# Zero rows fill the MLP's remainder tile, so that all gate and up matmuls contract over 128 rows

## The chip, the core and the metric

The kernel runs on one core of one Trainium2 chip. The time is the device time of one launch in microseconds (us). Work is done by five engines with queues of their own: TensorE (PE, with its weight loads listed as PEld), VectorE (DVE), ScalarE (ACT), GpSimd (POOL) and SyncE (SP), which issues most transfers. ACT issues some transfers too.

## The reference

One transformer block with adaptive layer norm, one sequence of 2048 tokens, width D = 576, MLP width F = 4608, all in float32:

```python
mod = (silu(c) @ w_mod).reshape(1, 6, 1, 576)
sa, ca, ga, sb, cb, gb = (mod[:, i] for i in range(6))
h = layernorm(x) * (1 + ca) + sa
x = x + ga * attention(h)            # 32 heads, 16 key/value heads, last 512 cached positions
h = layernorm(x) * (1 + cb) + sb
gate, up = h @ W_gate, h @ W_up      # [2048, 576] @ [576, 4608]
return x + gb * ((max(gate, 0) * up) @ W_down)
```

## The kernel before

**Precision.** TensorE's inputs are of a rounded float32 type (`F32R`). An operand is kept as a high part (the rounded value) and a low part (what the rounding left), and a product is made of three: high x high, low x high, high x low.

**The MLP.** The contraction runs over the 576 channels. Gate and up are computed by a scheme of seven products in place of eight (Strassen's: `P1` to `P7`), so each of its halves has 288 channels: two tiles of 128 rows and a remainder of 32. There are 36 blocks (`m`), 18 over the first half of the tokens (the first pass) and 18 over the second, seven products in each, and for each product a matmul group for gate and one for up (`xx`). `prod` (line 943) issues a group: for each of the two tiles of 128 the three products of high and low parts, then one matmul for the remainder. That one holds all three in a single stack of rows: weights low, high, high against activations high, high, low, 32 rows each, which makes 96. The weights' tiles (`wop`, from `w_split` and `w_later`) have a fourth group of 32 rows with the high part once more; it is there, but not used.

**The activations.** The normed activations of the second layer norm are written to memory (`hb`, line 237), by `hb_store` (line 240). Its fifth part, the remainder, is stored three times over, 32 rows each, so that a load gives 96 rows. `hb_load` (line 250) loads a tile. From those loads the seven sums of the scheme (`B11`, `B21`, `B22`, `T1` to `T4`) are built for the first half of the tokens by `h0_load`, `h0_comb`, `h0_hi` and `h0_cut`, and for the second by `h_later`, which runs in the first pass beside the MLP; both split into high and low, and the rows 64 to 95 of a remainder become the low part. The results go to memory (`hkeep`) except three that stay on chip, and `h_back` reloads them as `hop` tiles, five transfers for each operand. Four operands are reloaded for the first pass, and seven for the second, all at the end of the first.

**Order.** PE, DVE, ACT and POOL execute in the order in which the program is written; attention's is written as steps with times (ten to a unit, 128 units), the MLP's as slots, seven to a block. In a slot stand one product of gate and up and one or two pieces of down projection (`md_piece`, line 599, 12 matmuls of 288 columns; `st_tile`, line 1045, 6 matmuls, in the second pass). SP's transfers follow the order of the program as well, and each waits in the queue for what it needs. Weights of the first pass are cut into high and low on the chip for each slot (`w_split`, lines 720 to 722) and kept; the second pass reloads them (`wop<-wk_P`, line 735). `w_sums` (line 750) makes sums of raw weights on DVE; line 610 adds a finished piece of down projection to the result.

Of the kernel before, what the change touches and what calls it, by code (L numbers as in the profile page):

```python
# [7 lines left out]
F32 = mybir.dt.float32  # L8
F32R = mybir.dt.float32r
# [5 lines left out]
P = 128  # L15
S = 2048
D = 576
# [5 lines left out]
NQB = S // 512  # L23
# [10 lines left out]
def kernel(  # L34
# [13 lines left out]
    nc = tc.nc  # L48
# [18 lines left out]
    dr = ctx.enter_context(tc.tile_pool(name="dr", bufs=1, space=bass.MemoryType.DRAM))  # L67
# [144 lines left out]
    def prep_out(d, k, src, key, slot=None, at=(None, "wC")):  # L212
# [11 lines left out]
        def cut():  # L224
# [9 lines left out]

    hT = [None] * NQB

    hb = {(qb, d): dr.tile([2, 3, 32, 512] if d == 4 else [P, 512], F32, name=f"hb{qb}_{d}")
          for qb in range(NQB) for d in range(5)}

    def hb_store(qb, d, cols, f, eng=None):  # L240
        eng = eng or nc.sync
        if d < 4:
            eng.dma_start(hb[qb, d][:, cols], f)
            return
        for j in range(2):
            s = f[32 * j:32 * j + 32]
            eng.dma_start(hb[qb, 4][j, :, :, cols].rearrange("r p n -> p r n"),
                              s[:, None, :].to_broadcast([32, 3, s.shape[1]]))

    def hb_load(dst, qb, j, t):  # L250
        if t < 2:
            nc.sync.dma_start(dst, hb[qb, 2 * j + t])
        else:
            nc.sync.dma_start(dst[:96], hb[qb, 4][j].rearrange("r p n -> (r p) n"))

    h0, late = {}, []
    pend, pend_act = [], []
# [483 lines left out]
    def w_sums(m, s):  # L741

        r = {ij: wraw.get((m, *ij)) for ij in RAW}
        if s == "S2":
# [8 lines left out]

    TERMS = {"B11": "+00", "B21": "+10", "T2": "+11-01+00", "T3": "+11-01", "T1": "+01-00",
             "T4": "+10-11+01-00", "B22": "+11"}
    hkeep = {(b, s, k): dr.tile([96 if k == 2 else P, 512], F32R, name=f"hk{b}_{s}_{k}")
             for b in range(2) for s in TERMS for k in range(5)}

    def terms_of(s, table):
        w = table[s]  # L760
        return [(w[i], int(w[i + 1]), int(w[i + 2])) for i in range(0, len(w), 3)]

    def h_later(b, s, t):

        st = {}
        n = 96 if t == 2 else P
        terms = terms_of(s, TERMS)

        def get(dst, j, k):
            hb_load(dst, 2 * b + k, j, t)  # L770

        def begin():
            if b:
                ab = wp.tile([P, 2, 512], F32, tag="wC", name=f"hx{b}_{s}_{t}")
                st["a"], st["b"] = ab[:, 0, :], ab[:, 1, :]
            else:
                for x in "ab":
                    st[x] = hp.tile([P, 512], F32, tag="hT", name=f"h{x}{b}_{s}_{t}")
            for x, term in zip("ab", terms):
                get(st[x], *term[1:])  # L780

        def comb(i):
            x, y = st["a"][:n], st["b"][:n]
            nc.gpsimd.tensor_tensor(x, x, y, op=ALU.add if terms[i][0] == "+" else ALU.subtract)  # L784
            if i + 1 < len(terms):
                get(st["b"], *terms[i + 1][1:])

        def cut():
            a = st["a"]
            hi = hp.tile([P, 512], F32R, tag="hT", name=f"hy{b}_{s}_{t}")  # L790
            nc.scalar.copy(hi[:n], a[:n])
            if t < 2:
                lo = st["b"].bitcast(F32R)
                nc.gpsimd.tensor_sub(lo, a, hi.bitcast(F32))
                stores.append((hkeep[b, s, 3 + t], lo))
            else:
                nc.gpsimd.tensor_sub(hi[64:96], a[64:96], hi[64:96].bitcast(F32))
            stores.append((hkeep[b, s, t], hi[:n]))

        return [begin] + [lambda i=i: comb(i) for i in range(1, len(terms))] + [cut]  # L800
# [6 lines left out]
    def h0_load(j, k, t):  # L807
        h0[j, k, t] = hp.tile([P, 512], F32, tag="hT", name=f"h0_{j}{k}{t}")
        hb_load(h0[j, k, t], k, j, t)

    def h0_comb(dst, a, b, op, t):
        n = 96 if t == 2 else P
        nc.vector.tensor_tensor(h0[(*dst, t)][:n], h0[(*a, t)][:n], h0[(*b, t)][:n], op=op)

    hy0 = {}

    def h0_hi(s, x, t):
        a, n = h0[(*x, t)], 96 if t == 2 else P
        hi = hy0[s, t] = hp.tile([P, 512], F32R, tag="hT", name=f"hy0_{s}_{t}")
        nc.scalar.copy(hi[:n], a[:n])  # L820

    def h0_here(s):
        for t in range(3):
            h0_hi(s, H0_CUT[s], t)
        for t in range(3):
            h0_cut(s, H0_CUT[s], t, True)

    def h0_cut(s, x, t, stay=False):
        a, n = h0[(*x, t)], 96 if t == 2 else P
        hi = hy0[s, t]  # L830
        if t < 2:
            lo = hy0[s, 3 + t] = hp.tile([P, 512], F32R, tag="hT", name=f"hz0_{s}_{t}")
            nc.gpsimd.tensor_sub(lo, a, hi.bitcast(F32))
        else:
            nc.vector.tensor_sub(hi[64:96], a[64:96], hi[64:96].bitcast(F32))
        if stay:
            if t == 2:
                hop[0, s] = [hy0[s, k] for k in range(5)]
            return
        if t < 2:  # L840
            stores.append((hkeep[0, s, 3 + t], lo))
        stores.append((hkeep[0, s, t], hi[:n]))

    def h_back(b, s):
        hs = hop[b, s] = [hp.tile([P, 512], F32R, tag="hT", name=f"hop{b}_{s}_{k}") for k in range(5)]
        for k in range(5):
            nc.sync.dma_start(hs[k][:96 if k == 2 else P].bitcast(F32), hkeep[b, s, k].bitcast(F32))


    WTERMS = {"P1": "+00", "P2": "+01", "P6": "+10+11-00", "P7": "+00-10", "P5": "+10+11", "P4": "+11",  # L850
# [83 lines left out]
    def prod(m, s, n, xx):  # L934

        hs, w = hop[m // NFP, OPS[s][1]], wop[n]
        ps = pair[m, s][:, xx, :]
        ops = []
        for t in range(2):
            ops += [(w[:, xx, t, :], hs[t]), (w[:, xx, 3 + t, :], hs[t]), (w[:, xx, t, :], hs[3 + t])]  # L940
        ops.append((w[0:96, xx, 2, :], hs[2][0:96]))
        for i, (a, c) in enumerate(ops):
            nc.tensor.matmul(ps, a, c, start=s not in heir(m) and i == 0 and s not in seeds_of(m), stop=i == len(ops) - 1,  # L943
                             skip_group_check=True)
# [164 lines left out]
    def heir(m):  # L1109
        return {"P2": "P1", "P3": "P5", **({"P4": "P7"} if 0 < m < NFP else {})}  # L1110

    def seeds_of(m):
        return ("P6", "P7") if 0 < m < NFP else ()
# [99 lines left out]
    def step(name, t, fn, *args):  # L1213
        sched.append((t + PLAN.get(name, 0), len(sched), fn, args))
# [14 lines left out]
    def setd(d, k, fn):  # L1229
        def go():  # L1230
            d[k] = fn()
        return go
# [119 lines left out]
    for i in range(1, first):  # L1352
        B = 80 * i
        for c, t, gap, a in (("q", 16, 5, 0), ("kv", 24, 5, 1), ("o", 44, 6, 2)):
            if parks[c] and i > a:
                key, d, pr = parks[c].pop(0)
# [7 lines left out]
    step("m3.col", 250, setd(mods, "b0", lambda: mod_col(3, 0.0)()))  # L1364
    step("m4.col", 400, setd(mods, "b", lambda: (mods["b0"], mod_col(4, 1.0)())))

    mkeep = dr.tile([P, D], F32, name="mkeep")

    def m5_back():
# [10 lines left out]
    for i, ab in enumerate(lay0 + lay):  # L1380
        n = i - len(lay0) - 2 * NFT + 4
# [125 lines left out]
    def after(t):  # L1507
        return next(x for x in calm if x >= t)

    t = 546  # L1510
    for s in ("P1", "P2", "P4", "P7", "P5", "P6", "P3"):
        for xx in range(2):
            for fn in w_later(s, xx, (xp, "xm", 640)):
                step("w.l", t, fn)
                t = after(t + 8)
# [18 lines left out]
    for t, s in ((1251, "B11"), (1257, "B21"), (1266, "T3")):  # L1534
        step("h.l", t, h_back, 0, s)
# [150 lines left out]
```

## Time and profile before

| | us |
|---|---|
| runs (3) | 2917.99 median, 2914.55 to 2919.14 |
| profiled execution, its own time | 2925.96 |
| its span, first to last instruction | 2923.5 |
| TensorE busy in it | 2858.1 |
| 0 to 1636 (mostly attention), TensorE busy | 1581.35 of 1636.00 |
| 1700 to 2290 (first pass of the MLP), TensorE busy | 584.10 of 590.00 |
| 2290 to 2840 (second pass), TensorE busy | 550.00 of 550.00 |

The mean granted clock of TensorE was 0.993 in that execution. In the profile, a row of grouped instructions gives line, engine, operation, output<-inputs by the program's names, shape, count, then busy time and mean nanoseconds of one, then the idle time of the engine before them with what ended it. A row of the timeline gives start, time taken, the same names, and how many alike in a row were merged. Matmuls overlap: one takes some 390 ns from start to its modelled end, and the next starts after some 227. The chain of waits is followed back from the last instruction, at each step to what released it.

### The profile page before, as it was taken

The numbers are of one execution on the slowest core, as the hardware profiler recorded it, in microseconds if no ns is written. First come the engines' busy times: TensorE is split into PE (matmuls) and PEld (weight loads), VectorE is DVE, ScalarE is ACT, GpSimd is POOL, SyncE is SP. The second block draws the span as 40 slices with busy tenths as digits, with TensorE's granted clock in tenths as the row PEclk, the third lists the DMA queues.
The fourth block names the chain that finished last, engine by engine and source line by source line (L and its number), as shares of the span: only waits on it lengthen the run. The fifth ranks groups of instructions, "written<-read, shape, count | busy, mean of one in ns | idle before, by whom it ended". The sixth has DMA issues, their size and how long they took to land. (4 is left out here: it accounts for less than half of the span.)

```text
span 2923.5 us, 41266 instructions
## 1 busy us (share of the span) xinstructions
PE 2858.1 (98%) x15214; PEld 2490.0 (85%) x15214; DVE 2161.4 (74%) x2981; ACT 1489.4 (51%) x2095; POOL 2117.4 (72%) x1564
## 2 busy tenths in 40 slices
PE   6799999999999999999999999999999999999999
PEld 4588888888888888888888888888888888888888
DVE  7888888888888888777889755666676466666666
ACT  4466666666676666666656444444444122222221
POOL 4588888888889889876778666777787356656553
PEclk9899999999999999999999999999999999999999
DMA  4011222222223223322144456666666944444443
GB/s 151 22 45 53 85 91 80 71 101 90 89 89 108 84 69 118 116 70 86 65 129 144 142 210 220 226 230 224 224 222 251 340 160 152 151 152 153 157 151 104
DMA packets 162697, 396.43 MB, mean 136 GB/s; under 512 B 14912, under 2 KB 61760, under 8 KB 162496
## 3 DMA queue, kind: packets, MB, share of 16 engines
q1 hardware_dynamic: 131472, 282.15, 30.2%
q10 hardware_dynamic: 31024, 111.65, 9.7%
q8 instruction: 120, 1.97, 0.3%
q14 instruction: 81, 0.66, 0.1%
HBM read 268.73 MB, written 153.32 MB: 144 GB/s over the span
## 5 line engine op out<-in xcount | busy, mean ns | idle before, releaser
L539 POOL TENSOR_TENSOR lo<-p,hi 128x1024 fp32r<-128x1024 f32 x256 | 610.0, 2405 | 1.1 <-ACT hi L519 1.1
L548 POOL TENSOR_TENSOR ks<-ks,p 128x512 f32<-128x512 f32 x256 | 344.0, 1344 | 271.8 <-ACT p L532 208.7
L460 DVE TRANSPOSE_TENSOR_REDUCE t<-s 128x32 f32<-128x1024 f32 x256 | 316.8, 1244 | 136.4 <-PE s L457 125.0
L943 PE MATMUL gu<-hop_B,wop 128*128 128x512 f32 (+1 forms) x1512 | 379.0, 394 | 0.9 <-DMA wop<-wk_P 0.9
L943 PEld LDWEIGHTS gu<-hop_B,wop 128*128 128x128 f32 (+1 forms) x1512 | 276.3, 188 | 53.6 <-issue 1.3
L383 PE MATMUL qps<-hTa,wA 128*128 128x512 f32 x1288 | 312.4, 394 | 9.7 <-ACT lfa L365 7.7
L943 PE MATMUL gu<-hop_T,wop 128*128 128x512 f32 (+1 forms) x1260 | 319.9, 393 | 0.0
L599 PE MATMUL wo<-woga,ohi 128*128 128x288 f32 x1472 | 305.9, 301 | 1.5 <-DVE lfa L363 1.5
L383 PEld LDWEIGHTS qps<-hTa,wA 128*128 128x128 f32 x1288 | 244.7, 190 | 62.1 <-ACT lfa L365 8.2
L530 DVE TENSOR_TENSOR p<-s,mb 128x1024 f32<-128x1024 f32 x246 | 290.3, 1219 | 4.1
L519 ACT CAST hi<-p 128x1024 fp32r<-128x1024 f32 x256 | 269.1, 1051 | 7.1
L599 PE MATMUL md<-wogb,hhi 128*128 128x288 f32 x1280 | 263.4, 298 | 5.8 <-DVE acc L610 4.9
L532 ACT ACTIVATE p<-p 128x1024 f32<-128x1024 f32 x246 | 259.9, 1056 | 8.0 <-DVE p L530 7.9
L943 PEld LDWEIGHTS gu<-hop_T,wop 128*128 128x128 f32 (+1 forms) x1260 | 228.4, 188 | 41.0
L610 DVE TENSOR_TENSOR acc<-md,acc 128x576 f32<-128x576 f32 x160 | 120.9, 756 | 177.5 <-PE md L599 177.1
L435 ACT ACTIVATE qhi<-qps 128x512 fp32r<-128x512 f32 x128 | 76.5, 598 | 341.1 <-PE qps L383 341.1
L599 PEld LDWEIGHTS wo<-woga,ohi 128*128 128x128 f32 x1472 | 238.7, 188 | 9.1 <-issue 1.9
L599 PEld LDWEIGHTS md<-wogb,hhi 128*128 128x128 f32 x1280 | 214.9, 190 | 19.1 <-DVE acc L610 6.3
L1054 DVE TENSOR_TENSOR acc<-st_P,acc 128x576 f32<-128x576 f32 x160 | 121.1, 757 | 133.7 <-PE st_P L1045 133.7
L599 PE MATMUL wo<-woga,olo 128*128 128x288 f32 x736 | 216.9, 295 | 0.3 <-POOL olo L588 0.2
L599 PE MATMUL md<-wogb,hlo 128*128 128x288 f32 x640 | 190.1, 297 | 0.0
L588 POOL TENSOR_TENSOR olo<-rb,ohi 128x512 fp32r<-128x512 f32 x128 | 167.3, 1307 | 23.6 <-ACT ohi L584 23.1
(269 smaller groups left out, 7106.6 us busy)
## 6 DMA issues: line engine op xcount, KB each, us to landing
wop<-wk_P SPq DMA_DIRECT2D x133, 640.0 KB
wk_P<-wop ACTq DMA_DIRECT2D x119, 640.0 KB
wr<-wlay SPq DMA_DIRECT2D x68, 384.0 KB
rogb<-wd SPq DMA_DIRECT2D x68, 288.0 KB
againq<-akq SPq DMA_DIRECT2D x18, 640.0 KB
rwA<-wq SPq DMA_DIRECT2D x32, 320.0 KB
wlay<-wg SPq DMA_DIRECT2D x36, 256.0 KB
roga<-wo SPq DMA_DIRECT2D x32, 288.0 KB
```

Of the source, the lines that this page charges most:

```text
L383: return [lambda i=i, a=a, b=b: nc.tensor.matmul(ps, a, b, start=(i == 0), stop=(i == n - 1)) for i, (a, b) in enumerate(ops)]
L460: nc.vector.tensor_reduce(t4[u][:, 2 * h:2 * h + 2, :].rearrange("p k b -> p (k b)"), t.rearrange("p k (b j) -> p (k b) j", j=32), axis=AX ...
L519: nc.scalar.copy(hi_[u, h], pt[u, h])
L530: nc.vector.tensor_tensor(p, t, bc[u][:, None, :].to_broadcast([P, 2, 512]), op=ALU.subtract)
L532: nc.scalar.activation(p, p, AF.Exp, bias=0.0, scale=1.0)
L539: nc.gpsimd.tensor_sub(lo_[u, h], pt[u, h], hi_[u, h].bitcast(F32))
L548: nc.gpsimd.tensor_tensor(ks_[u], ks_[u], p[:, j, :], op=ALU.add)
L588: nc.gpsimd.tensor_sub(olo[u], o.pop(u), ohi[u].bitcast(F32))
L599: nc.tensor.matmul(ps[:, half, :H2], a[:, sl], w[b][:, cs], start=(n == 0 and seed is None), stop=(n == 5), skip_group_check=seed is not None)
L610: nc.vector.tensor_tensor(av, ps[:, :, :H2], av, op=ALU.add)
L943: nc.tensor.matmul(ps, a, c, start=s not in heir(m) and i == 0 and s not in seeds_of(m), stop=i == len(ops) - 1, skip_group_check=True)
L1054: nc.vector.tensor_tensor(t, ps[:, :, :H2], t, op=ALU.add)
```

## The change

The stored remainder gets a fourth group of 32 rows. `hb_rest`, a new step at time 300 (unit 30 of attention), fills it with zeros, by eight transfers from a part of `wmod` that the launch code pads with zeros. `hb_load`, the sums and splits, `hkeep` and `h_back` handle 128 rows in place of 96, and the seventh matmul of every group contracts over 128 rows: the fourth group multiplies the repeated high part of the weights with zeros.

```diff
-    hb = {(qb, d): dr.tile([2, 3, 32, 512] if d == 4 else [P, 512], F32, name=f"hb{qb}_{d}")
+    hb = {(qb, d): dr.tile([2, 4, 32, 512] if d == 4 else [P, 512], F32, name=f"hb{qb}_{d}")
...
-            eng.dma_start(hb[qb, 4][j, :, :, cols].rearrange("r p n -> p r n"),
+            eng.dma_start(hb[qb, 4][j, 0:3, :, cols].rearrange("r p n -> p r n"),
...
+    def hb_rest():
+        for qb in range(NQB):
+            for j in range(2):
+                nc.sync.dma_start(hb[qb, 4][j, 3], wmod[0, 64:96, 4 * D:4 * D + 512])
...
-            nc.sync.dma_start(dst[:96], hb[qb, 4][j].rearrange("r p n -> (r p) n"))
+            nc.sync.dma_start(dst, hb[qb, 4][j].rearrange("r p n -> (r p) n"))
...
-    hkeep = {(b, s, k): dr.tile([96 if k == 2 else P, 512], F32R, name=f"hk{b}_{s}_{k}")
+    hkeep = {(b, s, k): dr.tile([P, 512], F32R, name=f"hk{b}_{s}_{k}")
...
-        n = 96 if t == 2 else P
+        n = P
...
-            nc.sync.dma_start(hs[k][:96 if k == 2 else P].bitcast(F32), hkeep[b, s, k].bitcast(F32))
+            nc.sync.dma_start(hs[k].bitcast(F32), hkeep[b, s, k].bitcast(F32))
...
-        ops.append((w[0:96, xx, 2, :], hs[2][0:96]))
+        ops.append((w[:, xx, 2, :], hs[2]))
...
+    step("hb.r", 300, hb_rest)
```

The line `n = 96 if t == 2 else P` changes in the same way in `h_later`, `h0_comb`, `h0_hi` and `h0_cut`. On PE, DVE, ACT and POOL every instruction stands where it stood. SP's queue is longer by eight rows. In unit 30 it reads, before (`wlay` is the relaid weights of the MLP, `wm` a part of the modulation weights, `rkv` and `roga` raw key/value and output weights; the brackets name what a row waits for):

```order
L189 DMA rwA_4441<-wq 128x640 [waits DMAHW4_49,DMAHW2_49,Pool_49]
L1383 DMA wlay<-wu 2x128x256 [waits DMAHW3_49]
L137 DMA wm_2_4566<-wmod 128x576 [waits DVE_49]
L1383 DMA wlay<-wg 2x128x256 [waits DMAHW5_49]
L203 DMA rkv_1_4597<-kv 128x512 [waits DMAHW6_49,DMAHW0_49,Pool_49]
```

and with the change (line numbers of the changed kernel):

```order
L189 DMA rwA_4441<-wq 128x640 [waits DMAHW4_49,DMAHW2_49,Pool_49]
L253 DMA hb_4_142<-wmod 32x512 [waits DMAHW3_49]
L253 DMA hb_4_142<-wmod 32x512
L253 DMA hb_4_147<-wmod 32x512 [waits DMAHW5_49]
L253 DMA hb_4_147<-wmod 32x512 [waits DMAHW6_49]
L253 DMA hb_4_152<-wmod 32x512 [waits DMAHW7_49]
L253 DMA hb_4_152<-wmod 32x512 [waits DMAHW0_49]
L253 DMA hb_4_157<-wmod 32x512 [waits DMAHW1_49]
L253 DMA hb_4_157<-wmod 32x512 [waits DMAHW2_49]
L1389 DMA wlay<-wu 2x128x256 [waits DMAHW3_49]
L137 DMA wm_2_4574<-wmod 128x576 [waits DMAHW4_49,DVE_49]
L1389 DMA wlay<-wg 2x128x256 [waits DMAHW5_49]
```

The eight transfers of zeros stand ahead of a `wlay` copy and of `wm`, each waiting for the earlier transfer that used its semaphore. The second place is the reload of an operand at the end of the first pass, on SP, before:

```order
L847 DMA hop_T_0_22755<-hk_T_0_372 128x512 [waits DMAHW6_49,Pool_49]
L847 DMA hop_T_1_22756<-hk_T_1_373 128x512 [waits DMAHW7_49,PE_49]
L847 DMA hop_T_2_22757<-hk_T_2_374 96x512 [waits DMAHW0_49,PE_49]
L847 DMA hop_T_3_22758<-hk_T_3_375 128x512 [waits DMAHW2_49,PE_49]
L847 DMA hop_T_4_22759<-hk_T_4_376 128x512 [waits DMAHW3_49,PE_49]
L735 DMA wop_22753<-wk_P_158 128x1280 [waits DMAHW4_49,PE_49]
```

and with the change:

```order
L852 DMA hop_T_0_22763<-hk_T_0_372 128x512 [waits DMAHW6_49,Pool_49]
L852 DMA hop_T_1_22764<-hk_T_1_373 128x512 [waits DMAHW7_49,PE_49]
L852 DMA hop_T_2_22765<-hk_T_2_374 128x512 [waits DMAHW0_49,PE_49]
L852 DMA hop_T_3_22766<-hk_T_3_375 128x512 [waits DMAHW2_49,PE_49]
L852 DMA hop_T_4_22767<-hk_T_4_376 128x512 [waits DMAHW3_49,PE_49]
L740 DMA wop_22761<-wk_P_158 128x1280 [waits DMAHW4_49,PE_49]
```

The rows and their waits are the same; the third transfer is of 128 rows in place of 96.

More of the change, by code (lines that the diff above doesn't have):

```diff
@@ L811, in h0_comb @@
     def h0_comb(dst, a, b, op, t):
-        n = 96 if t == 2 else P
+        n = P
         nc.vector.tensor_tensor(h0[(*dst, t)][:n], h0[(*a, t)][:n], h0[(*b, t)][:n], op=op)
@@ L817, in h0_hi @@
     def h0_hi(s, x, t):
-        a, n = h0[(*x, t)], 96 if t == 2 else P
+        a, n = h0[(*x, t)], P
         hi = hy0[s, t] = hp.tile([P, 512], F32R, tag="hT", name=f"hy0_{s}_{t}")
@@ L828, in h0_cut @@
     def h0_cut(s, x, t, stay=False):
-        a, n = h0[(*x, t)], 96 if t == 2 else P
+        a, n = h0[(*x, t)], P
         hi = hy0[s, t]
```

## The prediction

> **What bounds the kernel now.** First the page of the profile: the share of each engine, and the span in forty slices.
>
> ```profile
> PE 2858.1 (98%) x15214; PEld 2490.0 (85%) x15214; DVE 2161.4 (74%) x2981; ACT 1489.4 (51%) x2095; POOL 2117.4 (72%) x1564
> PE   6799999999999999999999999999999999999999
> PE 29%; POOL 2%; DMA 2%; DVE 1%; issue 1%; ACT 1%; ACTq 0%; SPq 0%; POOLq 0%; DVEq 0%
> ```
>
> TensorE is busy 98% of the span, and 9 tenths or more in every slice after the second. The change touches the MLP, which the matmuls of line 943 (1512 of them on `hop_B` alone) place from about 1636 us on. So the next view is the busy time by stage.
>
> ```profile
> core 0: us, PE busy (x) PEld busy (x) DVE busy (x) ACT busy (x) POOL busy (x), PEclk, DMA share, GB/s
> 1700.00:2290.00 590.00, 584.10 (x3197) 514.24 (x3196) 378.84 (x361) 253.28 (x353) 434.63 (x377) 0.99 0.64 231
> 2290.00:2840.00 550.00, 550.00 (x2952) 481.38 (x2953) 345.50 (x478) 129.46 (x243) 306.09 (x301) 1.00 0.51 170
> ```
>
> In the second pass of the MLP (2290 to 2840) TensorE has no idle time at all; in the first it has 590.00 - 584.10 = 5.9 us. What TensorE's own stream saves therefore comes off the end, except where something else holds it back. Where that is, the chain of waits tells, asked for 1876 to 2290 and then for 2290 to the end (it cannot be followed back past 1876).
>
> ```profile
> by line: PE gu L943 32.2%; PE md L599 20.4%; POOL wop L722 7.0%; issue 6.0%; POOL wop L721 3.8%; DVE ws L750 3.3%; DMA wk_P<-wop 3.0%; DVE wr L750 2.9%; DMA rogb<-wd 2.3%; DMA hx_T<-hb 2.3%; ACT wop L720 2.2%; DMA wop<-wk_P 2.0%; POOL hx_T
> by line: PE gu L943 64.5%; PE st_P L1045 28.5%; PE md L599 5.6%; DVE acc L610 0.2%; DVE su L1054 0.1%; DVE gu L1091 0.1%; DVE q L1092 0.1%; DVE acc L1066 0.1%; DVE q L1090 0.1%; issue 0.0%; DVEq L1091 0.0%; DVEq L610 0.0%
> ```
>
> In the second pass 98.6% of the chain is TensorE. In the first pass it is 52.6%; the other 47.4% of 414 us, about 196 us, runs through the cutting of weights on POOL, sums on DVE and transfers. TensorE is nearly always busy there too, but a faster TensorE would only wait a little longer at the next hand-over.
>
> **The matmul with fewer rows.** Each product of the MLP is seven matmuls into one bank, six with 128 rows and the last with 96. There are 36 blocks x 7 products x 2 (gate and up) = 504 of the last kind.
>
> ```profile
> L943 PE MATMUL gu<-hop_B,wop 128*128 128x512 f32 x1296 | 334.7, 393 | 0.9 <-DMA wop<-wk_P 0.9
> L943 PE MATMUL gu<-hop_B,wop 96*128 96x512 f32 x216 | 85.3, 395 | 0.0
> L383 PE MATMUL qps<-hTa,againq x504: 387/389/481, 1184.0 to 1617.4; 128*128 128x512 f32 x168
> ```
>
> Fewer rows buy nothing: 395 ns mean against 393 for its neighbours. And both stand above the 389 ns median of the same 128x512 form in the q projection, where no matmul has 96 rows. Ends of matmuls are modelled, so spacing of starts is the better measure. The timeline has a place where a 96-row matmul is followed by twelve of 128 rows and of the same width, with no wait between (second column: time taken, overlapping the next).
>
> ```profile
> 1648.48 0.39 PE L943 MATMUL gu<-hz_T,wop 128*128 128x512 f32 x1
> 1648.71 0.40 PE L943 MATMUL gu<-hy_T,wop 96*128 96x512 f32 x1
> 1648.94 0.40 PE L572 MATMUL pv<-hi,againv 128*128 128x512 f32 x1
> 1649.18 0.40 PE L573 MATMUL pv<-hi,againv 128*128 128x512 f32 x1
> 1649.41 0.39 PE L574 MATMUL pv<-lo,againv 128*128 128x512 f32 x1
> 1649.64 0.39 PE L572 MATMUL pv<-hi,againv 128*128 128x512 f32 x1
> ...
> 1651.45 0.39 PE L574 MATMUL pv<-lo,againv 128*128 128x512 f32 x1
> ```
>
> From 1649.64 to 1651.45 lie eight spacings: 1.81 / 8 = 0.2263 us each. From the 96-row matmul at 1648.71 to 1649.64 lie four: 0.93 us, that is 0.93 - 4 x 0.2263 = 0.025 us more. Getting into the 96 rows costs nothing (0.23); getting out disturbs that matmul and the next three. Is it the rows, or merely that one accumulation ends and the next begins with other operands? In attention the scores end and the q projection begins in another bank, all with 128 rows:
>
> ```profile
> 1002.05 0.39 PE L457 MATMUL s<-qlo,kv 128*128 128x512 f32 x1
> 1002.27 3.34 PE L383 MATMUL qps<-hTa,wA 128*128 128x512 f32 x14
> 1005.46 0.35 PE L483 MATMUL qm<-t,quad 128*128 128x80 f32 x2
> ```
>
> 0.22 us across the boundary, and fourteen in 3.19 us (0.228, the last being one before another change of form). So a boundary as such is free, and I put the 25 ns down to the change of rows. Two products in a row in the MLP, a piece of the chain, bear it out:
>
> ```profile
> 1980.56 3.22 PE gu L943 x14
> ```
>
> 3.22 us less 14 x 0.2263 = 3.17 leaves 0.05, twice 25 ns, and there are two 96-row matmuls in it. The page "TensorEngine Tiling (Array Packing)" of the Trainium skill says in its Key Properties that changing the tiling mode drains the engine; 96 rows is none of the modes that it lists, and it gives no time, so the sum does not use it, but the disturbance on leaving the 96 rows would be of that kind.
>
> **The price of one removal.** I take 26 ns: the 25 above, read to 10 ns, agrees with that within its rounding. The bounds come from the rest. Most of the 504 are followed not by matmuls of 512 columns but by a piece of down projection with 288, and whether the three disturbed spacings go away there is less sure:
>
> ```profile
> 2503.18 0.43 PE L1045 MATMUL st_P<-sw_B,sh_A 128*128 128x288 f32 x2
> ...
> 2503.99 1.79 PE L943 MATMUL gu<-hop_T,wop 128*128 128x512 f32 x7
> 2505.61 0.43 PE L1045 MATMUL st_P<-sw_B,sh_A 128*128 128x288 f32 x2
> 1007.29 0.39 PE L572 MATMUL pv<-hi,kv 128*128 128x512 f32 x1
> ...
> 1008.89 0.39 PE L573 MATMUL pv<-hi,kv 128*128 128x512 f32 x1
> ...
> 1010.03 0.42 PE L599 MATMUL wo<-woga,ohi 128*128 128x288 f32 x2
> ...
> 1010.82 0.29 PE L599 MATMUL wo<-woga,ohi 128*128 128x288 f32 x1
> ```
>
> In the MLP six of 288 columns and seven of 512 take 0.81 + 1.62 = 2.43 us; in attention, with 128 rows throughout, six take 0.79 and the first seven after such a piece take 1.60: 2.39. The difference, about 40 ns for each removal, is the upper bound; the lower is the 96-row matmul's own excess alone, 395 - 389 = 6 ns. So 504 removals save 504 x 0.026 = 13.1 us, at least 3.0 and at most 20.2. The seventh matmul itself goes on costing one spacing, as 128 rows do.
>
> **What is given back.** Three terms, all in the first pass.
> - Over the MLP (1636 to the end, 1287 us) 13.1 us is a rate of 1.0%. Where the chain is not TensorE's, 196 us, that gain becomes waiting: -2.0 us.
> - Before 1876 the chain is unknown for 240 us, worth 2.4 us; lost between nothing and all of it, I take half: -1.2 us.
> - Each of the eleven reloads of a cut operand from memory, and each load that builds one, carries 128 rows of 2 KB in place of 96, 64 KB more. It matters where transfers hold TensorE, which is at the end of the first pass, where seven reloads stand in one run of SP's queue:
>
> ```profile
> 2200.00:2290.00 90.00, 88.97 (x488) 78.11 (x487) 57.60 (x53) 36.15 (x50) 67.70 (x57) 1.00 0.78 280
> 2273.44 6.61 DMA hop_B<-hk_B
> 2281.46 8.29 DMA wop<-wk_P
> ```
>
> There the chain leaves TensorE for `hop_B` and then `wop`, and the 0.9 us wait quoted above on line 943 follows. Some four reloads lie ahead of that `wop`: 4 x 64 KB at the 280 GB/s of this stretch is 0.9 us; with what TensorE saves meanwhile, -1.0 us. Between 0 (the transfers have other slack) and 7 x 64 KB, 1.6 us.
>
> **What costs nothing, and its cover.** The eight new transfers of zeros (64 KB each) are put into SP's queue ahead of a `wlay` copy, in unit 30 of attention:
>
> ```profile
> 435.50 0.59 SPq L1383 DMA_DIRECT2D wlay<-wu  x1
> 443.12 0.34 SPq L137 DMA_DIRECT2D wm<-wmod  x1
> ```
>
> SP has nothing to issue from 436.1 to 443.1, 7.0 us, and eight issues of 0.34 to 0.59 take 2.7 to 4.7 us. Behind them stand that copy, `wm`, and the next key/value and output weights; if the cover were gone, they would be late by some 3 us at most, once, with TensorE waiting for no more than that. The casts and sums on 128 partitions in place of 96 take the same time:
>
> ```profile
> L784 POOL TENSOR_TENSOR hx_T<-hx_T 128x512 f32<-128x512 f32 x14 | 18.0, 1284 | 2.4 <-DMA hx_T<-hb 2.1 <-DMA rogb<-wd 0.3
> L784 POOL TENSOR_TENSOR hx_T<-hx_T 96x512 f32<-96x512 f32 x7 | 9.0, 1285 | 2.1 <-DMA hx_T<-hb 2.0
> ```
>
> **Sum.** 13.1 - 2.0 - 1.2 - 1.0 = 8.9, say 9 us. The profiled execution spans 2923.5 us and took 2925.96, so 2.5 us lie around it; it would span 2914.5. The median of the runs is 2917.99, 8 us below that execution; the same 9 us off it give 2909.
>
> **Rivals.**
> - *The count of rows does not matter, or only the 6 ns do.* For it: 395 against 393 ns, hardly a difference, and the spacing after a piece of 288 columns is disturbed in attention too (1.60 us where seven undisturbed take 1.58). Against it: the place at 1648.71, where nothing but the rows changes width or form, and the free boundary at 1002.27. Gain 3.0 less some of the 4.2 given back: 2918, or 2916 to 2919. By the page "TensorE: Matmul & The Clock Gate" of the Trainium skill, section "Why this matters for your kernels", one matmul with 32 contraction rows takes the same time as one with 128: by that rule filling the rows changes nothing and the time stays 2918. The rows agree for the matmul by itself, and speak against it for the three behind.
> - *More than forecast.* All of the 40 ns go, 20.2 - 4.2 = 16 us, or the two collisions told of next vanish: 2899 to 2902. For it: the comparison of 2.43 with 2.39 us. Against it: the pattern after a piece of 288 columns depends on where the piece ended, and need not become attention's.
> - *Slower, by collisions on DVE.* DVE's sum of raw weights at line 750 normally takes 0.95 us, but sometimes several times that while POOL works, and behind it stands the add of a down projection piece for which TensorE waits.
>
> ```profile
> 2029.04 6.06 DVE L750 TENSOR_TENSOR wr<-wr,wr 128x768 f32<-128x768 f32 x1
> PE md L599 <- DVE acc L610: 4.9, 3, 2.3
> L750 DVE TENSOR_TENSOR wr<-wr,wr x17: 945/948/6064, 1667.7 to 2248.1; 128x768 f32<-128x768 f32 x17
> ```
>
> Three such waits cost 4.9 us now, two of them about 2.3 each. One block in 17 or so more or less is a matter of how TensorE's hand-overs fall against POOL's work, and the change moves TensorE by 0.36 us a block (14 x 26 ns). Were the long wait to come in every one of the 17 blocks, 15 more at 2.3 us would be 34 us: 2909 + 34 = 2943. It decides from four (which eat the 9 us) and makes the kernel slower beyond doubt from seven more: about 2925. Against it: the pattern has been struck only three times while the blocks already differ from one another.
>
> **How the numbers follow.** Forecast 60%, with its own range 2903 to 2914; no effect or 6 ns only 18%; more than forecast 10%; collisions 12%. The measurement can tell 0.2%, 5.8 us, from no change. Of the forecast 56 parts lie beyond that and 4 within; the second case lies within; the third beyond; of the last 10 are slower and 2 within. Faster 0.66, the same 0.24, slower 0.10. For the range I go down to 2900, which leaves out about half of the third case, and up to 2919, which takes in all of the second and leaves out the slower ones: some 15% outside.
>
> **What would show it.** Right: all 3528 matmuls of line 943 have 128 rows with a mean nearer 390 than 393, fourteen in a row take 3.19 us or less where they take 3.22, seven and six in the second pass take 2.40 in place of 2.43, and the stretch to the end shrinks by about 6 to 9 us there, less in the first pass. Wrong in the price: line 943 keeps its 393 mean. Wrong in what is given back: TensorE's idle time in 1700 to 2290 grows by more than 4 us, by line 610 (collisions) or by `wop` and `hop` (transfers). Wrong about the cover: TensorE idles near 440 to 470 us, where it does not now.

## The result, and the profile after

The kernel with the change takes 2903.68 us (median of 5 runs, 2902.66 to 2907.59); the kernel before, beside it on the same chip, 2918.01 (5 runs, 2914.55 to 2922.9). The ratio is 0.9952, with a 95% interval of 0.9941 to 0.9963: faster by 0.4 to 0.6%. A second measurement of the same pair, later, gave 2907.04 against 2918.39, ratio 0.9962 (0.9948 to 0.9975). So the gain is 14.3 us in the one and 11.4 in the other. The profiled execution took 2907.59 and spans 2905.8.

| us | before | after |
|---|---|---|
| span of the profiled execution | 2923.5 | 2905.8 |
| TensorE busy in it | 2858.1 | 2845.2 |
| first to last matmul of gate and up on `hop_B` | 1266.4 | 1248.8 |
| first pass, 1700 to 2290, TensorE without work | 5.9 | 3.1 |
| the three waits of the MLP on `acc`, in all | 4.9 | 2.6 (two) |

The page of the changed kernel, engines and the chain of waits as shares of the span:

```profile
PE 2845.2 (98%) x15214; PEld 2481.1 (85%) x15214; DVE 2162.0 (74%) x2981; ACT 1489.1 (51%) x2095; POOL 2114.7 (73%) x1564
PE 90%; DVE 4%; POOL 3%; ACT 1%; issue 1%; DMA 1%; SPq 0%; ACTq 0%; POOLq 0%; DVEq 0%
L948 PE MATMUL gu<-hop_B,wop 128*128 128x512 f32 x1512 | 374.8, 391 | 0.3 <-POOL wop L727 0.2
```

As many matmuls as before, 15214, in 12.9 us less of TensorE's time; the other engines execute as many instructions as before. All 1512 of this group have 128 rows now, with a mean of 391 ns in place of 393 and 395. That is not yet the gain, since their ends are modelled: it lies in where the next one starts. The same stages as before, by busy time of each engine (the columns are the same too):

```profile
1700.00:2290.00 590.00, 586.93 (x3246) 516.18 (x3245) 381.91 (x364) 254.69 (x355) 433.53 (x377) 1.00 0.67 241
2290.00:2840.00 550.00, 550.00 (x2994) 484.21 (x2993) 353.72 (x490) 132.59 (x249) 315.21 (x309) 1.00 0.51 168
```

In 550.00 us of a TensorE that is never idle, in both kernels, 2994 matmuls start where 2952 did: 1.4% more. (The window holds other places of the program, so the two counts compare rates only roughly.) What the waits of the MLP are (in all, times, longest):

```profile
PE md L604 <- DVE acc L615: 2.6, 2, 2.4
PE md L604 <- issue: 0.9, 1, 0.9
PE gu L948 <- POOL wop L727: 0.6, 3, 0.2
```

Before, the waits for `acc` came to 4.9 us in three; one of 0.9 us for the reloaded `wop` is gone here, and the waits for POOL's `wop` went from 0.2 us to 0.6. None is new. The place that gave the price, products at the start of the MLP followed by matmuls of the same width, in the timeline of the changed kernel:

```profile
1647.30 0.39 PE L948 MATMUL gu<-hy_T,wop 128*128 128x512 f32 x1
1647.53 0.39 PE L577 MATMUL pv<-hi,againv 128*128 128x512 f32 x1
1647.75 0.39 PE L578 MATMUL pv<-hi,againv 128*128 128x512 f32 x1
1647.98 0.39 PE L579 MATMUL pv<-lo,againv 128*128 128x512 f32 x1
1648.20 0.39 PE L577 MATMUL pv<-hi,againv 128*128 128x512 f32 x1
...
1650.02 0.39 PE L579 MATMUL pv<-lo,againv 128*128 128x512 f32 x1
```

The four spacings behind the seventh matmul take 1648.20 - 1647.30 = 0.90 us where they took 0.93, and the eight after them 1650.02 - 1648.20 = 1.82 where 1.81 was read, the same within the rounding. And in the second pass, seven of 512 columns and six of 288:

```profile
2485.59 0.42 PE L1050 MATMUL st_P<-sw_B,sh_A 128*128 128x288 f32 x2
...
2486.39 1.76 PE L948 MATMUL gu<-hop_B,wop 128*128 128x512 f32 x7
2487.99 0.42 PE L1050 MATMUL st_P<-sw_B,sh_A 128*128 128x288 f32 x2
```

0.80 + 1.60 = 2.40 us in place of 2.43.

To sum such differences over the whole MLP, from its first matmul of gate and up to the last matmul of the program, I took the starts of all of TensorE's matmuls in the trace and added up by how much each spacing stands above the bare one (227 ns after a matmul of 512 columns, 132 after one of 288), for spacings less than 16 ns above; larger ones are counted apart, as waits. I call the first sum the **disturbance**. Before it is 18.8 us, after 6.3: 12.5 us less. With a bound of 30 ns in place of 16 the two sums are 18.8 and 6.4, so the bound decides nothing. The larger gaps come to 13.6 us before and 8.5 after.

### The profile page after: what moved, and what is told of

It is laid out like the page before. It is cut to its first block, busy times and chain, and to the rows that moved or that the text cites. A ratio compares the mean times of both kernels' runs of the same rounds, so it can differ in the third digit from the quotient of the medians.

```text
span 2905.8 us, 41275 instructions
## 1 busy us (share of the span) xinstructions
PE 2845.2 (98%) x15214; PEld 2481.1 (85%) x15214; DVE 2162.0 (74%) x2981; ACT 1489.1 (51%) x2095; POOL 2114.7 (73%) x1564
## 4 chain that ended last, share of the span: by engine, by line
PE 90%; DVE 4%; POOL 3%; ACT 1%; issue 1%; DMA 1%; SPq 0%; ACTq 0%; POOLq 0%; DVEq 0%
PE gu L948 26%; PE wo L604 13%; PE qps L388 13%; PE md L604 8%; PE st_P L1050 6%; PE s L461 4%; PE s L462 4%; PE s L460 4%; PE pv L579 4%; PE pv L578 4%; PE pv L577 4%; PE qm L488 1%; POOL lo L544 1%; DVE ws L755 0%; DVE hTa L376 0%
## 5 line engine op out<-in xcount | busy, mean ns | idle before, releaser
L948 PE MATMUL gu<-hop_B,wop 128*128 128x512 f32 x1512 | 374.8, 391 | 0.3 <-POOL wop L727 0.2
L948 PEld LDWEIGHTS gu<-hop_B,wop 128*128 128x128 f32 x1512 | 274.9, 188 | 51.0 <-POOL wop L727 0.9
L948 PE MATMUL gu<-hop_T,wop 128*128 128x512 f32 x1260 | 316.1, 391 | 0.0
L948 PEld LDWEIGHTS gu<-hop_T,wop 128*128 128x128 f32 x1260 | 227.9, 188 | 38.9
```

## The experiments

Below, "gate and up" is the time from the first to the last matmul of gate and up on `hop_B`, which begins after attention and so leaves out what attention varies by; its rows are at the end of this section. Theories A to D are named in the expectations. Each kernel was timed beside the kernel before.

**Undo the rows of the seventh matmul alone.** Everything else of the change stays: the zeros, the 128 rows of loads, sums and reloads.

```diff
-        ops.append((w[:, xx, 2, :], hs[2]))
+        ops.append((w[0:96, xx, 2, :], hs[2][0:96]))
```

> The changed kernel with one thing undone: the seventh matmul of each group contracts over 96 rows again; zeros, 128-row loads, sums and reloads stay. Theory A (each step from a 96-row matmul to a 128-row one disturbs the stream): back to the time of before, 2918 give or take 4, ratio 0.999 to 1.001; six and seven matmuls in the second pass 2.43 us again. Theory C (the gain came from the other parts of the change, such as fuller transfers or other meetings of DVE and POOL): stays near 2904, ratio 0.995. The eight transfers of zeros and the longer reloads by themselves: at most 1 us.

2919.16 us (11 runs) against 2918.32, ratio 1.0006 (0.9998 to 1.0015). Its disturbance is 18.8 us, that of before to the tenth. The timeline in the second pass is the one of before:

```profile
2499.24 0.43 PE L1050 MATMUL st_P<-sw_B,sh_A 128*128 128x288 f32 x2
...
2500.05 1.79 PE L948 MATMUL gu<-hop_T,wop 128*128 128x512 f32 x7
2501.67 0.43 PE L1050 MATMUL st_P<-sw_B,sh_A 128*128 128x288 f32 x2
```

0.81 + 1.62 = 2.43. So the whole gain comes from 504 matmuls having 128 rows in place of 96, and theory C falls: the zeros, the wider sums and the larger transfers together cost at most 0.15% (4 us), and bring nothing that shows.

**A second matmul with 96 rows in each group.** In the kernel before, the third of the seven gets 96 rows too.

```diff
+        ops[2] = (ops[2][0][0:96], ops[2][1][0:96])
         ops.append((w[0:96, xx, 2, :], hs[2][0:96]))
```

> The kernel before with a second matmul of each group on 96 rows, the third (it leaves out 32 rows of weights high x activations low in the first tile). Theory A: 504 more steps from 96 to 128 rows, each followed by three more matmuls of 512 columns, at 25 to 26 ns: 13 us slower than before, 2931, ratio 1.0045. Theory B (a matmul with fewer rows costs its own 6 ns, whatever stands beside it): 3 us slower, 2921. Theory C: 2918.

2922.77 us (10 runs), ratio 1.0015 (1.0006 to 1.0024): slower by 4.5 us. The disturbance grows from 18.8 to 27.4 us, 8.6 more or 17 ns for each of the 504. Fourteen matmuls of two products in a row show it:

```profile
1647.35 3.42 PE L944 MATMUL gu<-hop_B,wop 128*128 128x512 f32 x14
1650.60 0.29 PE L483 MATMUL qm<-t,quad 128*128 128x16 f32 x2
```

3.25 us from the first to what follows; the same fourteen take 3.21 in the kernel before and 3.18 in the changed one. The doses add, in the direction of theory A, but over the MLP the second costs two thirds of what A expected, for which no run gives the reason. The median shows half of the 8.6. In its profiled execution TensorE waited less (larger gaps of 3.7 us in all, the fewest in the table below), so the slower stream may have filled waits that were there anyway; that is one profile, and not shown.

**All seven with 96 rows.** Every matmul of gate and up loses its last 32 rows, so that the rows never change inside a group. The MLP's result is incomplete; the run is there for its time alone.

```diff
         for i, (a, c) in enumerate(ops):
+            a, c = a[0:96], c[0:96]
```

> The kernel before with all seven matmuls of each group on 96 rows (it leaves out a quarter of the rows of the first six, so the MLP's result is incomplete). Theory A: no steps within or between adjacent groups; those from a group to a piece of down projection stay (385 of 504). So 119 x 26 ns = 3 us faster than before, 2915, spacings of 227 ns inside the groups. Theory B: 3024 more matmuls at 6 ns or more, at least 18 us slower, 2936 or above. Theory C: 2918.

2909.32 us (6 runs), ratio 0.9968 (0.9957 to 0.9979), disturbance 7.3 us. Here A was wrong: many steps from 96 rows to 128 remain, one wherever down projection follows gate and up (375 in the trace), and they cost almost nothing: 1.0 us of disturbance more than the changed kernel in all.

```profile
2483.71 1.76 PE L944 MATMUL gu<-hop_B,wop 96*128 96x512 f32 x7
2485.31 0.42 PE L1046 MATMUL st_P<-sw_B,sh_A 128*128 128x288 f32 x2
...
2486.10 1.76 PE L944 MATMUL gu<-hop_B,wop 96*128 96x512 f32 x7
```

1.60 and 0.79: the 2.39 of attention, although the rows change twice in each cycle. What these steps have in common is that the width changes with the rows, from 512 columns to 288. That led to A': a change of rows starts a disturbance as a change of width does; where both fall together it adds nothing.

The same run has one place with the two steps apart from each other and from any change of width: gate and up, then twelve matmuls of 128 rows, then gate and up again, all with 512 columns.

```profile
1646.25 0.39 PE L944 MATMUL gu<-hy_T,wop 96*128 96x512 f32 x1
1646.48 0.40 PE L572 MATMUL pv<-hi,againv 128*128 128x512 f32 x1
...
1649.00 0.39 PE L574 MATMUL pv<-lo,againv 128*128 128x512 f32 x1
1649.22 3.37 PE L944 MATMUL gu<-hop_B,wop 96*128 96x512 f32 x14
1652.43 0.29 PE L483 MATMUL qm<-t,quad 128*128 128x16 f32 x2
```

Spacings in ns, from the starts in the trace: on the way out 233, 235, 229, 232, 231, then 227; on the way in 232, 236, 228, 233, 231, then 226. Five of 226.7 make 1133, so it is 27 ns out and 27 in (1160 each). Getting into the 96 rows costs as much as getting out. A single 96-row matmul has both steps one spacing apart, and pays once.

**The 96-row matmul first in its group.** The same 504 matmuls as before, each at the head of its group.

```diff
-        ops.append((w[0:96, xx, 2, :], hs[2][0:96]))
+        ops.insert(0, (w[0:96, xx, 2, :], hs[2][0:96]))
```

> The kernel before with the 96-row matmul first in its group in place of last (another order of the same sum). Theory A: the disturbed spacings (233, 237, 233, 231 ns) move to the group's first four matmuls, the seventh takes 227, and the pieces of 288 columns behind it fall to the 0.79 us that six take without it; time 2915 to 2920, since there are as many steps. A rival D (the end of an accumulation and the change of bank disturb, not the rows): the disturbance stays behind the seventh matmul, and 2918.

2907.69 us (5 runs) against 2918.32, ratio 0.9962 (0.9948 to 0.9975): 10.6 us of gain with every 96-row matmul still there, and 11.3 of the 12.5 us of disturbance gone. The timeline:

```profile
1648.87 3.40 PE L943 MATMUL gu<-hop_B,wop 96*128 96x512 f32 x14
...
2485.25 1.76 PE L943 MATMUL gu<-hop_B,wop 96*128 96x512 f32 x7
2486.85 0.42 PE L1045 MATMUL st_P<-sw_B,sh_A 128*128 128x288 f32 x2
```

Behind a piece with 288 columns the seven take 1.60 us, as in the changed kernel; the disturbance over the MLP is 7.5 us, 1.2 above the changed kernel's, and what is left of it sits in the groups that follow matmuls of the same width, where the steps fall in mid-stream (233, 237, 233, 231 ns, then 226). A in its simple form is gone, and so is B (the 6 ns of fewer rows are still paid here). D is gone too: behind the seventh matmul, where the accumulation ends, the spacing is 227 ns. A' holds.

**Order alone, with 128 rows.**

```diff
-        ops.append((w[:, xx, 2, :], hs[2]))
+        ops.insert(0, (w[:, xx, 2, :], hs[2]))
```

> The changed kernel with the remainder matmul first in its group, on 128 rows: the order alone. Theories A and A': nothing moves, 2904, give or take 2; the block lengths of the change within 0.05 us. If the order were what helped in the run with 96 rows first: below 2902.

2905.22 us (4 runs), ratio 0.9958 (0.9945 to 0.9972), disturbance 5.9 us. Putting the remainder first by itself changes nothing that shows, so what the run before gained came from where the step of rows falls.

**96 rows only right behind a piece of down projection, else 128.** From the changed kernel, by A': put every step at a change of width or just behind one, and none into mid-stream. `piece_last` is set to true at the head of `down_piece` and of `st_tile`.

```diff
...
-        ops.append((w[:, xx, 2, :], hs[2]))
+        n = 96 if piece_last[0] else P
+        piece_last[0] = False
+        ops.insert(0, (w[:n, xx, 2, :], hs[2][:n]))
```

> The changed kernel with the remainder matmul first in its group, and on 96 rows only where a piece of 288 columns stands right before the group, 128 rows elsewhere. Theory A (every step from 96 to 128 rows costs 25 ns): some 385 steps come back, about 10 us slower than the change, 2914. Theory A' (a change of rows restarts a disturbance that a change of width starts anyway; where both fall together it adds nothing): no slower than the change, 2904; by the run with 96 rows first, where a piece and a group of seven in the first pass took 3.180 us against 3.198 with the change, up to 150 times 18 ns less: 2901.

2904.24 us (5 runs) against 2917.42, ratio 0.9953 (0.994 to 0.9965). The disturbance falls to 4.5 us, 1.8 below the changed kernel, and an undisturbed block of the first pass takes 34.96 us in place of 35.07. Theory A expected some 10 us more here, and it is refuted again: 383 matmuls have 96 rows. Against the run with all 504 first on 96 rows, this one is without the 121 that do not stand behind a piece, and its disturbance is 7.5 - 4.5 = 3.0 us less, some 25 ns for each of them: the price of a step in mid-stream once more. The medians do not separate this kernel from the change, so the two were put side by side, together with a second profile of the kernel before:

> The changed kernel, unchanged, beside the next one on one chip: 2903.7 again, ratio 0.995; the lengths of the blocks as in its first profile, the long waits perhaps at other places.

> The kernel with 96 rows first after a piece and 128 rows elsewhere, once more, beside the change. Its first profile had the MLP 2.3 us shorter than the change, but its median was no shorter. Theory A': 2901.4, ratio 0.9943. If the waits take the 2.3 us back: 2903.7.

The change 2907.04 (5 runs, ratio 0.9962), the mixed kernel 2905.55 (5 runs, ratio 0.9959, 0.9947 to 0.9971). Disturbance 6.2 and 4.7 us, as in the first pair. The 1.5 us are in the trace and not shown in the time: the profiled execution of the mixed kernel lost more than that at one reload, at the end of the first pass:

```profile
PE md L607 <- DVE acc L618: 2.9, 3, 2.4
PE gu L953 <- DMA wop<-wk_P: 2.6, 1, 2.6
```

Whether it beats the change stays open.

**The kernel before, once more**, to see what its profile varies by.

> The kernel before, unchanged, profiled once more: which of its waits return. If the long waits on VectorE's add (2.3 us each, near 1959 and 2033 us) belong to the program, both are there again; if they come and go from one execution to the next, one or both are missing and the span is 2 to 8 us shorter than 2923.5, with the lengths of the blocks in the second pass the same within 0.05 us.

One run of 2917.01 us; its span is 2915.2 where the other execution's is 2923.5. The disturbance is 18.8 us again, but the larger gaps fell from 13.6 to 8.8:

```profile
PE md L599 <- DVE acc L610: 2.7, 3, 2.3
PE md L599 <- issue: 0.9, 1, 0.9
PE gu L943 <- POOL wop L722: 0.2, 1, 0.2
```

One of the two 2.3 us waits for `acc` and the 0.9 us wait for `wop` are not there. Of the 8.3 us between the spans, 4.7 lie ahead of the MLP (gate and up begin at 1633.0 instead of 1637.7) and 5.0 in it, while the end behind the last matmul is 1.4 longer. So the pair of profiles overstates the change: 17.7 us between the spans, of which 12.5 are disturbance and 5.1 are larger gaps (13.6 - 8.5), and these come and go without any edit.

**Fewer rows yet.** From the changed kernel, the seventh matmul with 64 rows and with 32.

```diff
-        ops.append((w[:, xx, 2, :], hs[2]))
+        ops.append((w[0:64, xx, 2, :], hs[2][0:64]))
```

```diff
-        ops.append((w[:, xx, 2, :], hs[2]))
+        ops.append((w[32:64, xx, 2, :], hs[2][32:64]))
```

> The changed kernel with the last matmul of the group on 64 rows (it leaves out weights high x activations low of the remainder). Theories A and A' with a price that does not depend on the count: 2918, as with 96. A price that grows with the rows left out, or a drain because 64 rows are a mode of their own: more than 2922. No price for 64 rows: 2904.

> The same on 32 rows, the second group of the four (it leaves out both products of the remainder with a low part). Price independent of the count: 2918. Growing with it or a drain: more than 2922, and more than with 64 rows. None: 2904.

3095.56 us, ratio 1.0611 (1.0596 to 1.0625), and 3100.94, ratio 1.0627 (1.0611 to 1.0644): 192 and 197 us above the changed kernel, or 381 and 391 ns for each of the 504 matmuls. No theory had expected that size. Both kernels leave out products with a low part, so they too are there for their times alone. Weight loads of the kernel with 64 rows, then its matmuls (what stands in brackets is the idle time ahead of the load):

```profile
2699.38 1.23 PEld L948 LDWEIGHTS gu<-hop_B,wop 128*128 128x128 f32 x6
2700.97 0.18 PEld L948 LDWEIGHTS gu<-hop_B,wop 64*128 64x128 f32 x1 [0.35 <-issue]
2701.39 0.82 PEld L1050 LDWEIGHTS st_P<-sw_T,sh_S 128*128 128x128 f32 x6 [0.24 <-issue]
...
2699.51 1.95 PE L948 MATMUL gu<-hop_B,wop 128*128 128x512 f32 x7
2701.40 1.05 PE L1050 MATMUL st_P<-sw_T,sh_S 128*128 128x288 f32 x6
2702.28 1.95 PE L948 MATMUL gu<-hop_B,wop 128*128 128x512 f32 x7
```

Seven and six take 2702.28 - 2699.51 = 2.77 us instead of 2.40. The load with 64 rows comes 0.35 us after the sixth load has ended, and 0.32 us after the sixth matmul has started (2700.65 in the trace, with its modelled end at 2701.04); the next load with 128 rows comes late likewise, 0.24 us after the load ahead of it and 0.43 after the start of the 64-row matmul. In the trace of the 32-row kernel the two delays are the same, 0.32 and 0.43 us. In the changed kernel the loads run on without such gaps (1.46 us for seven), each starting some 3 ns after the matmul ahead of it and running beside it:

```profile
2486.26 1.46 PEld L948 LDWEIGHTS gu<-hop_B,wop 128*128 128x128 f32 x7
2487.86 0.32 PEld L1050 LDWEIGHTS st_P<-sw_B,sh_A 128*128 128x128 f32 x2
```

**All runs together.** The column of gate and up is last start less first start, from the rows of the groups on `hop_B`; three of them, of before, of before once more and of after (name, count, then min/median/max in ns, first and last start):

```profile
L943 PE MATMUL gu<-hop_B,wop x1512: 387/393/632, 1637.7 to 2904.1; 128*128 128x512 f32 x162, 96*128 96x512 f32 x27
```

```profile
L943 PE MATMUL gu<-hop_B,wop x1512: 387/393/500, 1633.0 to 2894.4; 128*128 128x512 f32 x162, 96*128 96x512 f32 x27
```

```profile
L948 PE MATMUL gu<-hop_B,wop x1512: 387/389/504, 1636.3 to 2885.1; 128*128 128x512 f32 x189
```

| kernel | median us | gate and up | disturbance | larger gaps |
|---|---|---|---|---|
| before | 2918.01 | 1266.4 | 18.8 | 13.6 |
| before, once more | 2917.01 (one run) | 1261.4 | 18.8 | 8.8 |
| change, seventh back to 96 | 2919.16 | 1262.0 | 18.8 | 9.4 |
| before, two with 96 | 2922.77 | 1265.0 | 27.4 | 3.7 |
| the change | 2903.68 | 1248.8 | 6.3 | 8.5 |
| the change, again | 2907.04 | 1250.3 | 6.2 | 10.3 |
| change, remainder first | 2905.22 | 1250.2 | 5.9 | 10.3 |
| before, remainder first | 2907.69 | 1251.5 | 7.5 | 10.0 |
| before, all with 96 | 2909.32 | 1249.6 | 7.3 | 8.4 |
| mixed | 2904.24 | 1247.7 | 4.5 | 9.4 |
| mixed, again | 2905.55 | 1251.7 | 4.7 | 13.1 |

The kernels with 64 and 32 rows are left out: their delays are larger than the bound. The disturbance goes with the kernel and repeats to 0.2 us. The larger gaps go with the execution: 8.8 and 13.6 for one kernel, 9.4 and 13.1 for another. Differences in the second column of times are these two together, within 0.3 us.

## Why the prediction was right, point by point

The forecast was 2909 (2900 to 2919); 2903.68 and 2907.04 lie in the range and on the side of the gain.

**What bounds the kernel: right.** TensorE's own stream. Its 12.5 us came off the end, as far as the times tell: 14.3 and 11.4 us in the two comparisons, 12.8 in their mean.

**The price of one removal: right in the sum, not in its parts, and that by luck.** The prediction took 504 x 26 ns = 13.1 us; the trace shows 12.5, or 25 ns on average. But the 25 ns of the one place are not the price at every place. A block (98 matmuls of gate and up) has 14 of them. In the second pass an undisturbed one takes, start to start, 33.50 us in place of 34.03, so 0.53 / 14 = 38 ns each, near the upper bound of 40; in the first 35.07 in place of 35.28, so 0.21 / 14 = 15 ns. The sum came out because these average to 26, and nothing in the prediction's working said that they would. How they differ shows in the cycles of the first pass (medians from the starts in the trace): twelve matmuls of 288 columns behind a group of seven took 1597 ns and take 1584, but a group of seven between two such pieces went from 1603 to 1609. As the prediction said of this risk, the pattern after a piece depends on where the piece ended, and there it came back longer; in the mixed kernel it is 1596. What decides between the longer and the shorter pattern was not found.

**The reason for the price: right for the place, wrong as a rule.** A change from 96 rows to 128, or back, costs 25 to 27 ns in an even stream. That getting in is free and getting out costs, as the prediction read it from the place at 1648.71, is refuted: with all seven at 96 rows each of the two steps costs its 27 ns. The spacing into the 96-row matmul is even, since the disturbance of the way in begins one spacing later; with a single 96-row matmul the way out falls just there, and the two were taken for one. And that each such step has a price is refuted by the two runs that keep the steps and lose the cost: at a change of width, or one matmul behind it, the disturbance is there already. One matmul ahead of a change of width, where the kernel before had most of its steps, it is not. What in the engine makes the disturbance no run shows.

**What is given back: the step that failed.** The prediction took 2.0 us off because 196 of 414 us of the chain in the first pass were not TensorE's, 1.2 for the part where no chain could be followed, and 1.0 for the larger reloads. That is 4.2 us. The runs showed about none of it: the undisturbed blocks of the first pass keep their 0.21 us each, 17 x 0.21 and 17 x 0.53 make 12.6 us in all, and the 12.5 us of disturbance became 14.3 and 11.4 us of time. The interval of the first comparison, 10.8 to 17.2 us, leaves out the 9 us of the forecast; that of the second, 7.3 to 15.2, does not. The larger gaps did not grow either (13.6, 8.8 and 9.4 us in three executions with the seventh on 96 rows at the end of its group, 8.5 and 10.3 with the change), though they vary by more than the 4.2. The chain's share was a bad measure. For the same stretch, 1876 to 2290, it reads now:

```profile
by line: PE gu L948 50.2%; PE md L604 29.0%; DVE ws L755 3.3%; POOL wop L727 2.9%; DMA rogb<-wd 2.3%; issue 1.8%; DVE wr L755 1.5%; ACT wop L725 1.4%; POOL wop L726 1.3%; DMA hx_T<-hb 1.1%; POOL hx_T L789 1.0%; POOL wogb L182 0.8%; DVE c L1
```

and in the second execution of the kernel before:

```profile
by line: PE gu L943 40.6%; PE md L599 24.0%; POOL wop L722 5.9%; issue 4.8%; POOL wop L721 3.2%; DMA rogb<-wd 2.9%; DMA wk_P<-wop 2.7%; DVE ws L750 2.3%; ACT wop L720 2.2%; POOL hx_T L784 1.7%; DVE wr L750 1.7%; POOL wogb L182 1.1%; DMA hx_
```

TensorE's share of the chain was 52.6% in the one execution of before, is 40.6 + 24.0 = 64.6% in the other, and 79.2% after. A chain followed back from the end goes through other engines wherever a hand-over was tight, even by nothing; what can be lost hangs on the waits that TensorE has, and these are few: 6.9 and 3.8 us in the whole MLP in the two executions of before and 4.1 after (the rows of waits), most of it in one or two long ones. My reading of it, which no run tried by itself: a gain ahead of such a wait is lost only as far back as the last moment at which the engine waited for is itself set by TensorE, and that is a block or less.

**The larger reloads: open.** TensorE's wait for the transfer of `wop` was 0.9, none, none, 1.3 and none in the five kernels or executions that store 96 rows (before twice, two with 96, the remainder first, all with 96), 0.4 us in their mean. With 128 rows stored it was none, 0.3, 0.6, 1.9, 1.0 and 2.6 in six (the change twice, the seventh back to 96, the remainder first, the mixed kernel twice), 1.1 in their mean. That leans towards a cost of 0.6 us, but single executions of one kernel differ by more; the run with the seventh matmul back at 96 rows bounds it, with all else, at 4 us.

**The zeros: right about the cover, wrong about their price.** SP's queue in unit 30:

```profile
433.44 0.33 SPq L189 DMA_DIRECT2D rwA<-wq  x1
433.81 6.01 SPq L253 DMA_DIRECT2D hb<-wmod  x8
439.87 0.63 SPq L1389 DMA_DIRECT2D wlay<-wu  x1
441.42 0.54 SPq L137 DMA_DIRECT2D wm<-wmod  x1
...
445.02 3.52 SPq L203 DMA_DIRECT2D rkv<-kv  x1
```

The last of these in the kernel before:

```profile
446.72 0.34 SPq L203 DMA_DIRECT2D rkv<-kv  x1
```

Eight issues took 6.01 us, 0.75 each, and not 2.7 to 4.7, so the hole of 7.0 us still held them. But SP pays behind them as well: the issue of `rkv` took 3.52 us where it took 0.34, and that of `roga`, some 8 us later, 2.29 where it took 0.34. Four more executions with the zeros show the same (3.2 to 3.7 and 2.0 to 2.5 us), and three more without them 0.34 for both. TensorE is busy for all of 430 to 480:

```profile
430.00:480.00 50.00, 50.00 (x271) 43.87 (x270) 40.15 (x62) 33.86 (x46) 41.92 (x26) 1.00 0.27 83
```

**The rivals.** The 6 ns alone: refuted, since the remainder put first keeps its 96 rows and has the gain. More than forecast: nearly the 40 ns were reached in the second pass and not in the first, so the sum of prices, 12.5 us, is near the forecast's 13.1 and far from this rival's 20.2; the gains of 14.3 and 11.4 us lie between the 9 and the 16, because about nothing was given back. Collisions on DVE: the place is real and its wait of 2.4 us is there after as well, but it comes once or twice in most executions, never in three, and twice and once for one kernel. The rule that a single matmul with 32 rows takes as long as one with 128 stands in the Trainium skill, "TensorE: Matmul & The Clock Gate", section "Why this matters for your kernels". Carried over to this stream, by which the time would have stayed at 2918, it does not hold: filling the 96 rows brought 11.4 and 14.3 us, and with 32 rows each costs 391 ns more. No run here shows one matmul on its own, of which the page speaks.

**The signs named.** Seven and six in 2.40: seen. Fourteen in a row in 3.19 or less: missed by a hundredth, 3.20 in the chain where they took 3.22. A mean nearer 390 than 393: 391. In the second pass 6 to 9 us less: from its first matmul of gate and up to its last 614.2 us became 605.3, 8.9 less. None of the signs of being wrong came: TensorE's idle time in 1700 to 2290 fell from 5.9 to 3.1 us.

## What to carry to other kernels

Price a matmul by the spacing of the starts behind it, over as many as it takes until the spacing is bare again, and at more than one place: the same edit was worth 15 ns in one loop and 38 in the other. Keep the row count of a dense stream constant, or, between 128 and 96, let it change only where the width changes as well or just behind that, not just ahead. Padding from 96 rows to 128 with zeros took TensorE no time here (227 ns from start to start with either), and a remainder moved to the head of its group brought most of the same gain. Take a chain's share of other engines for no measure of what a faster engine will lose: look at how long it waits, and at a second profile of the same kernel, before a wait of 2 us is put into a sum.

## What the runs showed of the hardware that was not expected

Three classes of row counts show up in this stream. 128 rows run at 227 ns. 96 rows run at 227 too; a step between 128 and 96, either way, costs some 27 ns spread over the next four or five spacings, and next to nothing where a change of width has just disturbed the stream. 64 and 32 rows cost 381 and 391 ns each more: the weight load starts 0.32 us behind the matmul ahead of it on the way in and 0.43 on the way out, where a 128-row load in the changed kernel starts 3 ns behind. The page "TensorEngine Tiling (Array Packing)" of the Trainium skill, Key Properties, says that a change of the tiling mode drains TensorE; under "Available Configurations" it lists modes of 128, 64 and 32 rows. The delays with 64 and 32 rows fit that and give it a price, 192 and 197 us for 504 matmuls; 96 rows have no such delay, so here they behave like 128.

Also not expected: the eight transfers of 32 rows from `wmod` took SP 0.75 us each to issue, where neighbours took 0.33 to 0.63, and two single issues behind them 3.52 and 2.29 us in place of 0.34.
